# Opening columns side by side, bank evictions by ScalarE, one softmax subtraction, and a turned weight order in a gated mix of linear attention and an MLP

## The chip, the cores and the metric

The kernel runs on one core of a Trainium2 chip. The metric is the time of one execution in device microseconds. The kernel before takes 503.98 us as the median of three runs (503.89 to 505.81).

The core's engines are TensorE (PE, the products), VectorE (DVE), ScalarE (ACT), GpSimd (POOL) and SyncE (SP, which issues most DMAs). All five run their own instruction rows and wait for each other through semaphores.

## The reference

For 2048 rows x of width 512 two branches are computed and mixed by a gate.

```python
g = sigmoid((x * gate_w).sum(-1, keepdims=True))
q, k, v = split(x @ wqkv)                          # 32 heads of 16
pq, pk = q_h @ w_phi[h], k_h @ w_phi[h]            # per head, 16x16
phi = concat(softmax(p), softmax(-p))              # over the 16, for pq and pk: 32 features a head
kv, z = phi_k^T v, sum over rows of phi_k
a = (phi_q @ kv / (phi_q . z + 1e-6)) @ wo         # branch A: linear attention
b = relu(x @ w1 + b1)**2 @ w2 + b2                 # branch B: 512 -> 1792 -> 512
out = g * a + (1 - g) * b
```

Everything is float32. The two softmaxes of a row of scores need, for each head, the largest of the 16 (for +p) and the smallest (for -p).

## The kernel before, in words

**Products.** An operand is kept as two float32r tiles, a rounded high part (name ending in h) and the rest (l). A product of two such operands is three matmuls of 128x128 by 128x512: high by high, high by low, low by high (`mm3`). Where the program says "a block of twelve", it is four pairs of tiles times three. x @ w1 and x @ (wk folded, wv) use a scheme of seven products in place of eight over 2 x 2 blocks: the table `PAIRS` names them p1 to p7, tiles X... are sums of blocks of x, and O0 to O3 are the four forms of the w1 tiles.

**Phase one.** For two halves r of the rows, `u_step` makes the hidden tiles: a column u = (r, g) is seven products into the banks uA, uE and one of uB0/uB1 (shown as uB). p1 opens the bank A, ScalarE copies it to B, p2 ends A; p5 opens E, ScalarE copies it to a tile ol, p6 goes on in B, VectorE writes B + ol into E, and so on. `hidden` adds the bias, takes relu and square on ScalarE (`row<-uA,b1c`, `row<-row`), and the tile goes to DRAM (`hkept`). Two tiles of each set, made by `plain`, take the ordinary way. `v_step` does the same for keys and values with the banks vA, vB, vE; `features` makes the softmaxes of the keys, and `kv_burst` adds phi_k^T v with 64 narrow matmuls into the bank kv. `fold` multiplies w_phi into wk (and, at the end of the phase, into wq) by 64 matmuls into the four banks vA, vB, vE, kv and four transposes on VectorE (`phiT<-...`).

In the opening, column (0,1) runs p1 and p2, then column (0,2) p1 and p2, both in the bank uA; two plain tiles follow, then the fold of wk, and then the remaining products of the two columns, the second one half behind the first, ahead of the stream of later columns.

**Phase two.** It goes through the four row blocks i, in the order `ORDER_B`. For each there are 14 steps, one for each 128 rows of w2: `h_ready` loads a hidden tile into the ring (four buffers of 512, shared by nearly all loads) and splits it into O0 or O1 (`O0h<-ring` on ScalarE, `O0l<-ring,O0h` on VectorE or GpSimd, two buffers each); `w2_ready` splits a tile of w2, once, into K... tiles; `down` gives four banks (uA, uE, uB0, uB1: one for each 128 rows of the block) three matmuls each, a block of twelve. At the 14th step `evict` (line 854) empties the four banks.

Between those steps stands branch A, for pairs p of row chunks. `do_q` is the query product, a block of twelve from the folded weight (tiles XS2..., XS3..., by `wq_ready`) into one of vA, vB, vE, kv, then `exps`, `sums`. `transposed` multiplies by the normaliser (`q_phi`; GpSimd's `ez`), transposes on VectorE (`tb<-e`), and lays the pieces of tb into phiT: four by ScalarE (`phiT<-tb`), twelve by DMA. `do_n` takes phiT times kv (`vE<-phiT,kvb`), `attend` the product with wo. `gates` computes g for a block, from x in its plain form (`xn`, one buffer, four products with row sums).

`exps` (line 617) takes max and min of each head out of the bank, subtracts twice (p - max, min - p, each 512 wide) into the halves of a tile of 1024, and takes one exponential of it.

**What sets the order.** The program doesn't emit its instructions as it is written. The class `Plan` (lines 131 to 344) records each operation, gives it a due time from a clock of the products as written, and then simulates the five engines with costs of its own (`lengths`); at each step the engine that can start first takes, of the operations that could start by then, the one with the earliest due time. Operations of `nc.either` go to VectorE or GpSimd, whichever is free. PE takes products by groups, in the written order, unless the first of the next few is not ready in the simulation. A load from DRAM may start at most HORIZON (45 us) before its due time. All is then issued from one line, so that every instruction carries line 344 in the profile and is told apart by the names of its tiles.

## Time and profile before

| what | us |
|---|---|
| median of three runs | 503.98 |
| the profiled execution's own time | 505.25 |
| its span in the trace | 503.5 |
| PE busy | 490.7 (97%) |
| DVE busy | 401.9 (80%) |
| ACT busy | 245.3 (49%) |
| POOL busy | 147.6 (29%) |

The page's times are microseconds from the span's start. A row of the timeline gives start, length, engine, operation, output<-inputs, sizes, and in brackets the idle time of that engine before it with what ended it ("<-ACT row": ScalarE's write to a row). A row of the windows gives the stretch, its length, then the busy time and instruction count of PE, PEld (weight loads), DVE, ACT, POOL, and at the end the clock granted to PE (1.00 is full), the busy share of the DMA engines and GB/s. In the page's groups a row ends with the busy sum, the mean in ns, and the engine's idle time ahead of the group. Phase one lasts to about 239 us of the span, phase two from there on.

### The profile page before, as it was taken

How to read it: one execution, taken by the hardware profiler on the slowest of the kernel's cores; microseconds unless marked ns; L12 is line 12 of the kernel's file. 1: busy time of each engine (PE TensorE's matmuls, PEld its weight loads, DVE VectorE, ACT ScalarE, POOL GpSimd, SP SyncE). 2: the span in 40 equal slices, each digit the busy share in tenths (PEclk: the TensorE clock that was granted, in tenths of full speed). 3: DMA queues.
4: the chain of work that ended last, by engine and by line, in shares of the span. 5: the costliest groups of instructions: out<-in, count | busy, mean ns of one | idle time of the engine just before them, and what ended most of it. 6: DMA issues, size and time to landing. Idle time of an engine off the chain costs nothing.

```text
span 503.5 us, 9473 instructions
## 1 busy us (share of the span) xinstructions
PE 490.7 (97%) x3538; PEld 392.3 (78%) x3538; DVE 401.9 (80%) x611; ACT 245.3 (49%) x403; POOL 147.6 (29%) x122
## 2 busy tenths in 40 slices
...
GB/s 285 403 390 313 384 256 181 278 61 214 154 127 170 284 252 109 231 269 178 224 167 92 135 296 161 91 87 259 119 101 167 142 92 83 93 172 87 109 2 83
DMA packets 56518, 91.87 MB, mean 182 GB/s; under 512 B 7192, under 2 KB 16664, under 8 KB 56472
## 3 DMA queue, kind: packets, MB, share of 16 engines
...
## 4 chain that ended last, share of the span: by engine, by line
PE 74%; DMA 9%; DVE 9%; SPq 3%; ACT 2%; issue 2%; ACTq 0%; DVEq 0%
PE uB L344 20%; PE uE L344 11%; PE uA L344 11%; PE vB L344 9%; PE vA L344 8%; PE vE L344 7%; PE kv L344 7%; SPq L344 3%; DVE e L344 2%; DMA ring<-hkept 2%; DMA KT11h<-in_xT 1%; DMA b2b<-in_b 1%; ACT row L344 1%; DMA KT20h<-in_w 1%; DMA KT21l<-in_w 1%
## 5 line engine op out<-in xcount | busy, mean ns | idle before, releaser
L344 POOL TENSOR_TENSOR ez<-e,vext 128x512 f32<-128x512 f32 x32 | 44.1, 1400 | 60.8 <-ACT e L344 56.9
L344 ACT ACTIVATE O1h<-ring 128x512 fp32r<-128x512 f32 x33 | 20.7, 626 | 53.9 <-PE uB L344 25.9
L344 ACT ACTIVATE e<-e 128x1024 f32<-128x1024 f32 x27 | 28.5, 1056 | 30.9 <-DVE e L344 30.6
L344 DVE TENSOR_REDUCE sm<-e 128x64 f32<-128x1024 f32 x27 | 32.8, 1214 | 8.4 <-ACT e L344 8.3
L344 ACT ACTIVATE O0h<-ring 128x512 fp32r<-128x512 f32 x33 | 20.6, 627 | 33.5 <-PE uB L344 18.7
L344 ACT ACTIVATE row<-row 128x512 f32<-128x512 f32 x56 | 34.9, 627 | 0.8
L344 ACT ACTIVATE phiT<-tb 32x512 f32<-32x512 f32 x32 | 20.2, 630 | 26.4 <-DVE tb L344 20.3
L344 POOL TENSOR_TENSOR O0l<-ring,O0h 128x512 fp32r<-128x512 f32 x15 | 21.2, 1412 | 24.4 <-ACT O0h L344 22.8
L344 DVE TENSOR_TENSOR O1l<-ring,O1h 128x512 fp32r<-128x512 f32 x22 | 18.2, 829 | 12.3 <-ACT O1h L344 12.2
L344 POOL TENSOR_TENSOR O1l<-ring,O1h 128x512 fp32r<-128x512 f32 x11 | 14.2, 1292 | 27.9 <-ACT O1h L344 20.0
L344 DVE TENSOR_TENSOR O0l<-ring,O0h 128x512 fp32r<-128x512 f32 x18 | 14.3, 792 | 8.3 <-ACT O0h L344 8.3
L344 DVE TENSOR_TENSOR e<-e,w 128x1024 f32<-128x1024 f32 x16 | 20.2, 1261 | 0.2
L344 DVE TENSOR_REDUCE dz<-ez 128x64 f32<-128x1024 f32 x16 | 19.2, 1201 | 0.9 <-POOL ez L344 0.9
L344 DVE STREAM_TRANSPOSE tb<-e 128x1024 f32<-128x1024 f32 x16 | 19.7, 1232 | 0.1
L344 DVE SCALAR_TENSOR_TENSOR xn<-xn,gwb 128x512 f32<-128x512 f32 x16 | 13.5, 843 | 7.1 <-DMA xn<-in_xn 6.3
L344 DVE RECIPROCAL r<-sm 128x64 f32<-128x64 f32 x32 | 17.5, 546 | 0.5
L344 POOL TENSOR_TENSOR ring<-ring,ring 128x256 f32<-128x256 f32 x5 | 5.0, 1002 | 41.5 <-DVE O0l L344 24.8
L344 DVE TENSOR_TENSOR e<-e,r 128x1024 f32<-128x1024 f32 x11 | 16.8, 1523 | 0.2
L344 DVE TENSOR_REDUCE mx<-vA 128x32 f32<-128x512 f32 x10 | 6.9, 687 | 11.4 <-PE vA L344 11.4
L344 POOL TENSOR_TENSOR ring<-ring 128x256 f32<-128x256 f32 x3 | 3.2, 1068 | 40.9 <-DMA ring<-in_w 40.9
L344 DVE TENSOR_REDUCE mx<-vB 128x32 f32<-128x512 f32 x14 | 9.5, 676 | 6.0 <-PE vB L344 6.0
L344 ACT ACTIVATE row<-row,b1c 128x512 f32<-128x512 f32 x13 | 9.3, 719 | 7.8 <-DVE row L344 7.8
...
## 6 DMA issues: line engine op xcount, KB each, us to landing
...
```

The lines of the kernel that those rows point to most:

```text
L344: call(*map(real, op.args), **{k: real(a) for k, a in op.kw.items()})
```

## The change

- *Opening*: columns (0,1) and (0,2) run side by side, product by product; the second one uses vB and vE in place of uA and uE. The third and fourth weight forms of column 2 lie in two tiles apart (`ASIDE`). The fold of wk comes behind the first two items of the later columns, in place of ahead of the first p5.
- *Gates*: loads of xn are no longer held to the horizon of 45 us.
- *Softmax*: `exps` makes one subtraction of 1024 that reads the bank twice by broadcast (p - max and p - min), and two exponentials of 512, the second with the factor -1.
- *Second phase*: the 14 tiles of w2 and of the hidden layer are taken in the order 2, 3, ..., 13, 0, 1 (`turned`).
- *Evictions*: a finished bank is copied by ScalarE, into the row or (with the factor 1-g) into a slot of the ring, and the addition follows on VectorE or GpSimd, from SBUF. The very last block adds from the bank as before.
- *Planner*: where VectorE or ScalarE would take an operation that is due over 5 us later, it looks for one that becomes ready while that would run and is due soon, and takes that first, waiting for it.

```diff
--- before.py
+++ after.py
@@ -155,7 +155,7 @@
         writes = [aps[0]] + ([kw["accum_out"]] if outs == 2 else [])
         reads = [a for a in aps[1:] if a is not kw.get("accum_out")]
         op.size = max(free_size(a) for a in aps)
-        op.early = method == "dma_start" and reads[0].space == DRAM
+        op.early = method == "dma_start" and reads[0].space == DRAM and reads[0].tensor.name != "in_xn"
         wide = [a for a in reads if free_size(a) > 1]
         op.two = method in ("tensor_tensor", "scalar_tensor_tensor") and len(wide) > 1 and all(a.space != PSUM for a in wide)
         for a in reads:
@@ -331,6 +331,12 @@
                 if s <= t + 1e-9:
                     able.append(op)
             op = min(able, key=lambda o: (o.due, o.n))
+            if e in ("vector", "scalar") and op.due > t + 5.0:
+                ahead = t + self.lengths(op, e)[1]
+                soon = [o for o in waiting[e] if t < o.ready < ahead and o.due < o.ready + 1.0]
+                if soon and op.method != "dma_start":
+                    op = min(soon, key=lambda o: (o.due, o.n))
+                    t = max(free[e], op.ready, lock if op.two else 0.0)
             for x in op.choices:
                 waiting[x].remove(op)
             launch(op, e, t)
@@ -464,10 +470,14 @@
 
 
 
-    def w_tiles(i):
+    def w_tiles(i, g=None):
+        if (g, i) in ASIDE:
+            return [operand(t)[:, :512 if i < 3 else 256] for t in ASIDE[g, i]]
         if i < 2:
             return [operand(f"O{i}{j}", 512, 2) for j in "hl"]
         return [operand(f"O{i}{j}", 512 if i == 2 else 256) for j in "hl"]
+
+    ASIDE = {(2, 2): ("KB211l", "KT31l"), (2, 3): ("KT21h", "KB111l")}
 
     def w_kept(g, i, j):
         return wkept4[g, j] if i == 3 else wkept[g, i, j]
@@ -489,7 +499,7 @@
     def w_ready(r, g, i):
         if (r, g, i) in st:
             return
-        t = st[r, g, i] = w_tiles(i)
+        t = st[r, g, i] = w_tiles(i, g if r == 0 else None)
         if r == 1 and g > 0:
             for j in range(2):
                 nc.sync.dma_start(ff(t[j]), w_kept(g, i, j))
@@ -527,7 +537,7 @@
     def u_step(u, p):
         r, g = u
         if p == "p1":
-            st["A", u] = banks["uA"]
+            st["A", u] = banks["vB" if u == (0, 2) else "uA"]
             uproduct(st["A", u], u, p, True, False)
             st["B", u] = turn("uB0", "uB1")
             nc.scalar.activation(st["B", u], st["A", u], AF.Copy)
@@ -535,7 +545,7 @@
             uproduct(st["A", u], u, p, False, True)
             hidden(2 * r, 2 * g, st["A", u])
         elif p == "p5":
-            st["E", u] = banks["uE"]
+            st["E", u] = banks["vE" if u == (0, 2) else "uE"]
             uproduct(st["E", u], u, p, True, False)
             t = st["t5", u] = buf("ol", 512, 2)
             nc.scalar.activation(t, st["E", u], AF.Copy)
@@ -616,15 +626,15 @@
 
     def exps(ps, tag="e"):
         pv = ps.rearrange("p (h f) -> p h f", f=DH)
-        mx, mn = small("mx", H), small("mn", H)
+        ends = small("ends", 2 * H).rearrange("p (h t) -> p h t", t=2)
         ef = buf(tag, 2 * D, 2 if tag == "e" else 1)
         e = ef.rearrange("p (h t f) -> p h t f", t=2, f=DH)
-        bc = lambda t: t.unsqueeze(2).to_broadcast([P, H, DH])
-        nc.vector.tensor_reduce(mx, pv, AX.X, ALU.max)
-        nc.vector.tensor_reduce(mn, pv, AX.X, ALU.min)
-        nc.vector.tensor_tensor(e[:, :, 0, :], pv, bc(mx), ALU.subtract)
-        nc.vector.tensor_tensor(e[:, :, 1, :], bc(mn), pv, ALU.subtract)
-        nc.scalar.activation(ef, ef, AF.Exp)
+        for t, op in enumerate((ALU.max, ALU.min)):
+            nc.vector.tensor_reduce(ends[:, :, t], pv, AX.X, op)
+        nc.vector.tensor_tensor(e, pv.unsqueeze(2).to_broadcast([P, H, 2, DH]), ends.unsqueeze(3).to_broadcast([P, H, 2, DH]),
+                                ALU.subtract)
+        for t, scale in enumerate((1.0, -1.0)):
+            nc.scalar.activation(e[:, :, t, :], e[:, :, t, :], AF.Exp, scale=scale)
         return ef.rearrange("p (h f) -> p h f", f=DH)
 
     def sums(e3):
@@ -750,6 +760,10 @@
             split(t, *hl, nc.either)
             st.setdefault("wb", []).append(hl)
 
+    def turned(f):
+
+        return (f + 2) % NF
+
     def w2_place(f, j):
         return f"K{KOPS[f // 2]}{f % 2}{j}"
 
@@ -757,14 +771,15 @@
 
         if ("w2", f) in st:
             return
-        src = load(slot(w2_place(f + 1, "l")) if f < NF - 1 else ring(), w2[f * P:(f + 1) * P, :])
+        src = load(slot(w2_place(f + 1, "l")) if f < NF - 1 else ring(), w2[turned(f) * P:(turned(f) + 1) * P, :])
         t = st["w2", f] = [operand(w2_place(f, j)) for j in "hl"]
         split(src, *t, nc.either)
 
     def h_ready(t):
         i, f = divmod(t, NF)
         hi, lo = st["h", t] = [operand(f"O{t % 2}{j}", 512, 2) for j in "hl"]
-        split(load(ring(), hkept[ORDER_B[i], f]), hi, lo, nc.either)
+        b, f = ORDER_B[i], turned(f)
+        split(load(ring(), hkept[b, f]), hi, lo, nc.either)
 
     def q_phi(n, e3, r):
         ez = buf("ez", 2 * D).rearrange("p (h f) -> p h f", f=DH)
@@ -851,13 +866,18 @@
         mm3(st["d"][c], st["h", t], st["w2", f], slice(c * P, (c + 1) * P), ALL, f == 0,
             f == NF - 1 or t == NB * NF - 3 and c == NC - 1)
 
-    def evict(n, d, s):
-        if ("f", n) in st:
+    def evict(n, d, s, last=False):
+        if ("f", n) not in st:
+            o = st["f", n] = row()
+            nc.scalar.activation(o, d, AF.Copy)
+            nc.either.tensor_tensor(o, o, st["b2b"], ALU.add)
+        elif last:
             o = st["f", n]
             nc.vector.scalar_tensor_tensor(o[:, s], d[:, s], rest[:, n:n + 1], o[:, s], ALU.mult, ALU.add)
         else:
-            o = st["f", n] = row()
-            nc.vector.tensor_tensor(o, d, st["b2b"], ALU.add)
+            t, o = ring(), st["f", n]
+            nc.scalar.activation(t, d, AF.Copy, scale=rest[:, n:n + 1])
+            nc.either.tensor_tensor(o, o, t, ALU.add)
 
 
 
@@ -890,9 +910,6 @@
                 x_split(0, op, kk)
         plain(1, 1, banks["vE"])
         plain(1, 0, banks["kv"])
-        wph = load(slot("KT40h"), wphi)
-        fold("k", wkT, [slot(t) for t in ("KT40l", "KT41h", "KT41l", "KB220h")], wph)
-        fetch_v()
         for kk in range(2):
             x_sums(0, kk)
 
@@ -943,14 +960,17 @@
     U1, U2 = (0, 1), (0, 2)
     x_ready(0, "S3")
     x_ready(0, "S4")
-    us = [(U1, "p5"), (U1, "p6"), (U1, "p7"), (U1, "p3"), (U2, "p5"), (U1, "p4"), (U2, "p6"), (U2, "p7"), (U2, "p3")]
-    us += u_stream([(0, g) for g in range(3, NPF)], U2)
-    run(us[:16])
+    run([(U1, "p5"), (U1, "p6"), (U2, "p5"), (U2, "p6"), (U1, "p7"), (U2, "p7"), (U1, "p3"), (U1, "p4"), (U2, "p3")])
+    us = u_stream([(0, g) for g in range(3, NPF)], U2)
+    run(us[:2])
+    fold("k", wkT, [slot(t) for t in ("KT40l", "KT41h", "KT41l", "KB220h")], load(slot("KT40h"), wphi))
+    fetch_v()
+    run(us[2:12])
     for op in ("B11", "T1", "T3", "B22", "T2", "B21", "T4"):
         for kk in range(2):
             k_ready(op, kk)
     vs = v_stream([(0, m, "kv") for m in range(NC)])
-    run(merged(us[16:], vs))
+    run(merged(us[12:], vs))
 
     x_fetch(1)
     x_fetch2(1)
@@ -1016,10 +1036,10 @@
             continue
         for c in range(NC):
             n = ORDER_B[i] * NC + c
-            evict(n, st["d"][c], ALL)
+            evict(n, st["d"][c], ALL, last)
             if last and c == NC - 1:
                 for e, d, s in zip((nc.sync, nc.scalar), ends, halves):
-                    evict(n, d, s)
+                    evict(n, d, s, last)
                     e.dma_start(out[n * P:(n + 1) * P, s], st["f", n][:, s])
             else:
                 out_done(n)
```

PE in the opening, where the first two columns begin. The names: uA, vB, vE are banks, XA... tiles of x (half 0 is row block A11, XA12 is A12), O0 and O1 the weight forms; a number behind _ counts versions (different ones are different contents). Before:

```order
L344 MATMUL vE<-XA221l_228,O1h_156 128x512
L344 MATMUL vE<-XA221h_217,O1l_158 128x512
L344 MATMUL uA<-XA120h_149,O0h_172 128x512
L344 MATMUL uA<-XA120l_152,O0h_172 128x512
L344 MATMUL uA<-XA120h_149,O0l_186 128x512
L344 MATMUL uA<-XA121h_163,O0h_172 128x512
L344 MATMUL uA<-XA121l_167,O0h_172 128x512
L344 MATMUL uA<-XA121h_163,O0l_186 128x512
L344 MATMUL uA<-XA110h_134,O0h_165 128x512
L344 MATMUL uA<-XA110l_138,O0h_165 128x512
```

And in the changed kernel, at the same part of the program:

```order
L350 MATMUL uA<-XA111h_140,O0h_172 128x512
L350 MATMUL uA<-XA111l_145,O0h_172 128x512
L350 MATMUL uA<-XA111h_140,O0l_185 128x512
L350 MATMUL vB<-XA110h_134,O0h_165 128x512
L350 MATMUL vB<-XA110l_138,O0h_165 128x512
L350 MATMUL vB<-XA110h_134,O0l_177 128x512
L350 MATMUL vB<-XA111h_140,O0h_165 128x512
L350 MATMUL vB<-XA111l_145,O0h_165 128x512
L350 MATMUL vB<-XA111h_140,O0l_177 128x512
L350 MATMUL uA<-XA120h_149,O0h_172 128x512
L350 MATMUL uA<-XA120l_152,O0h_172 128x512
```

The other column's first six matmuls now go to vB and stand between the first and the second six of the column in uA; before, both columns took uA one after the other.

PE where the phases meet: the last products of phase one (uB), the last burst (kv, 32 matmuls for each of two row chunks), and what follows. XS2... is the folded query weight, KB110 the first tile of w2 that is used, O0 its hidden tile. Before:

```order
L344 MATMUL uB_72<-XA221h_1583,O3l_2745 128x512
L344 MATMUL kv<-ez_2542,vext_98 32x32 x32
L344 MATMUL kv<-e_2738,vext_99 32x32 x32
L344 MATMUL vA<-XS20h_2959,XA110h_1371 128x512
L344 MATMUL vA<-XS20l_2967,XA110h_1371 128x512
```

In the changed kernel:

```order
L350 MATMUL uB_72<-XA221h_1569,O3l_2737 128x512
L350 MATMUL kv<-ez_2526,vext_98 32x32 x32
L350 MATMUL kv<-e_2718,vext_99 32x32 x32
L350 MATMUL uA<-KB110h_2488,O0h_2846 128x512
L350 MATMUL uA<-KB110l_2495,O0h_2846 128x512
L350 MATMUL uA<-KB110h_2488,O0l_2855 128x512
L350 MATMUL uE<-KB110h_2488,O0h_2846 128x512
L350 MATMUL uE<-KB110l_2495,O0h_2846 128x512
L350 MATMUL uE<-KB110h_2488,O0l_2855 128x512
L350 MATMUL uB_72<-KB110h_2488,O0h_2846 128x512
```

Behind the burst the first tile's block of twelve comes ahead of the first query product, where the query product came first; the rows on vA follow behind the six of uB_72 and uB_73.

The evictions at the end of the first row block. VectorE before (row is the output tile, rest is 1-g, b2b the bias, tb, dz, sm, mx parts of branch A):

```order
L344 TENSOR_REDUCE dz_3567<-ez_3533 128x64
L344 SCALAR_TENSOR_TENSOR row_3542<-uA,rest,row_3542 128x512
L344 TENSOR_TENSOR row_3582<-uE,b2b_3036 128x512
L344 TENSOR_TENSOR row_3588<-uB_72,b2b_3036 128x512
L344 TENSOR_TENSOR row_3596<-uB_73,b2b_3036 128x512
L344 TENSOR_REDUCE mx_3605<-vB 128x32
```

ScalarE in the changed kernel:

```order
L350 ACTIVATE e_3476<-e_3476 128x32x16 x2
L350 ACTIVATE phiT_3525<-tb_3450 32x2x256 x4
L350 ACTIVATE ring_3551<-uA,rest 128x512
L350 ACTIVATE row_3557<-uE 128x512
L350 ACTIVATE row_3566<-uB_72 128x512
L350 ACTIVATE row_3572<-uB_73 128x512
L350 ACTIVATE e_3562<-e_3562 128x32x16 x2
```

The four banks leave by ScalarE, behind two exponentials and four copies of a transposed tile, where VectorE emptied them behind branch A's reductions.

## The prediction, made before the changed kernel had run

> **What bounds the kernel now.** I read the page first: the busy row of its first part.
>
> ```profile
> span 503.5 us, 9473 instructions
> PE 490.7 (97%) x3538; PEld 392.3 (78%) x3538; DVE 401.9 (80%) x611; ACT 245.3 (49%) x403; POOL 147.6 (29%) x122
> ```
>
> TensorE (PE) is busy 97% of the span, and the change takes no product away. So all it can win lies in the 12.8 us in which PE does nothing, and in the time in which PE works slowly. Next, therefore, the timeline of PE. Its rows with idle time in brackets are all the waits after the first microsecond.
>
> ```profile
> 19.25 0.50 PE L344 MATMUL uA<-XA110h,O0h 128*128 128x512 f32 x1 [1.59 <-ACT row L344]
> 30.62 0.50 PE L344 MATMUL uB<-XS30h,O2h 128*128 128x512 f32 x1 [0.86 <-DVE uE L344]
> 48.45 0.50 PE L344 MATMUL uB<-XS30h,O2h 128*128 128x512 f32 x1 [1.12 <-DVE uE L344]
> 238.28 0.76 PE L344 MATMUL kv<-e,vext 128*32 128x32 f32 x64 [0.41 <-DVE e L344]
> 240.89 0.80 PE L344 MATMUL vA<-XS20h,XA110h 128*128 128x512 f32 x1 [1.85 <-ACT XS20h L344]
> 287.97 0.37 PE L344 MATMUL vE<-phiT,kvb 64*32 64x256 f32 x1 [1.89 <-DMA phiT<-tb]
> 377.33 0.47 PE L344 MATMUL uA<-KB110h,O0h 128*128 128x512 f32 x1 [0.79 <-DVE row L344]
> ```
>
> Seven waits: 3.57 us in the opening, 2.26 where the two phases meet, 1.89 at the first transposed pair, 0.79 at the second end of a block: 8.51 us. The other 4.3 us stand at the two ends of the program, which the change leaves alone. Then the windows, for the granted clock (the PEclk number, third from the right).
>
> ```profile
> 240.00:246.00 6.00, 5.10 (x11) 3.72 (x12) 4.75 (x8) 4.24 (x8) 0.00 (x0) 0.56 0.76 223
> 246.00:252.00 6.00, 6.00 (x25) 4.80 (x25) 4.81 (x10) 2.37 (x4) 3.03 (x2) 0.88 0.71 196
> 288.00:294.00 6.00, 6.00 (x45) 4.26 (x46) 6.00 (x8) 1.60 (x3) 1.07 (x1) 0.72 0.89 297
> ```
>
> Behind the two longest waits the clock falls. The loss is (1 - 0.56) x 6 + (1 - 0.88) x 6 = 3.36 us behind the wait of 1.85, and (1 - 0.72) x 6 = 1.68 us behind that of 1.89. Behind 1.59 it doesn't fall. So a ceiling follows: 8.51 + 3.36 + 1.68 = 13.55 us, if every wait goes and none comes.
>
> The unit for all that follows is a block of twelve products, from the chain of waits: 2.74 us, or 0.228 a product.
>
> ```profile
> 299.04 2.76 PE vA L344 x12
> 301.80 2.73 PE vB L344 x12
> ```
>
> **The opening.** Its waits are for single-bank reuse and for VectorE (DVE).
>
> ```profile
> 18.52 0.68 ACT L344 ACTIVATE row<-uA,b1c 128x512 f32<-128x512 f32 x1
> 28.96 0.68 DVE L344 STREAM_TRANSPOSE phiT<-kv 128x512 f32<-128x512 f32 x1
> 29.87 0.70 DVE L344 TENSOR_TENSOR uE<-uB,ol 128x512 f32<-128x512 f32 x1 [0.23 <-PE uB L344]
> 47.71 0.69 DVE L344 TENSOR_TENSOR uE<-uB,ol 128x512 f32<-128x512 f32 x1
> ```
>
> The first: column two can't begin in uA until ScalarE (ACT) has read column one (18.52 + 0.68). Now it lies in vB, and between two touches of a bank by PE stand six products of the other column, 1.37 us, or more: gone. The second and third: a bank uB gets its next product only after DVE's addition, one row later on PE. With two columns side by side, another column's product stands between, 1.37 us against waits of 0.86 and 1.12: gone. What is new: the fold (64 rows) moves behind the first two columns, and its four transposes, some 2.4 us on DVE, now hold up the additions there. I walked PE from 8.90 at 0.228 a product: the fold falls at about 38, its transposes end at about 43, and the copy uB<-uA of the fifth column, queued on ACT behind the first split of the folded weight, comes about 0.5 us late near 49. Bounds: 0, and 1.59 (the longest wait of this stretch). Term: 3.57 - 0.5 = 3.1. The loads of w_phi and wk that move back on SP's queue are needed 12 us later than before, those of w1 that move up come sooner; they cost nothing, and if one were late it would show as a wait on DMA ahead of the fold.
>
> **Where the phases meet.** Before, PE's next work is the query product on the folded weight, whose last transpose, split and subtraction are these:
>
> ```profile
> 239.29 0.67 DVE L344 STREAM_TRANSPOSE phiT<-vE 128x512 f32<-128x512 f32 x1
> 239.70 0.61 ACT L344 ACTIVATE O1h<-ring 128x512 fp32r<-128x512 f32 x1
> 240.22 0.61 ACT L344 ACTIVATE XS20h<-phiT 128x512 fp32r<-128x512 f32 x1
> 240.96 0.68 DVE L344 TENSOR_TENSOR XS20l<-phiT,XS20h 128x512 fp32r<-128x512 f32 x1
> 243.28 0.63 ACT L344 ACTIVATE O0h<-ring 128x512 fp32r<-128x512 f32 x1 [0.88 <-DMA ring<-hkept]
> 234.56 1.30 POOL L344 TENSOR_TENSOR O0l<-ring,O0h 128x512 fp32r<-128x512 f32 x1 [1.62 <-DMA KT41l<-in_w]
> 236.71 0.61 ACT L344 ACTIVATE KT40h<-KT41l 128x512 fp32r<-128x512 f32 x1
> ```
>
> The other work, the first hidden tile, came only at 243.28, because it was the last one written. With tile three first, that tile was written long ago; its split stands on ACT where KT40h stood (236.71), its subtraction on POOL takes 1.30, so it is there at about 239.0, just when the second burst ends (it starts at 238.28, lasts 0.76, and loses its wait of 0.41: between 238.6 and 239.0). Twelve products, 2.74 us, then cover the query's wait of 1.85. KB221l leaves DVE's row ahead of the scaled e, so the 0.41 goes too. With the wait its clock loss goes. New: up to 0.6 if the POOL half is late; I take 0.3. Term: 2.26 + 3.36 - 0.3 = 5.3.
>
> The Trainium skill ("TensorE: Matmul & The Clock Gate", Part 1, What's actually happening) says that the array falls to half rate after an idle window of about 3.4 us, on a free-running window. The lengths agree (6.7 and 3.4 us at half clock by the windows above), the threshold doesn't: gaps of 1.85 and 1.89 were enough, and the trace decides.
>
> **The first transposed pair.** PE gets to it later by one query block and sooner by one tile: from the end of the first query product 11 tiles and 3 queries stand before it, now 10 and 4, 14 blocks either way. So the chain to it must become shorter by itself.
>
> ```profile
> 246.13 0.63 PE L344 MATMUL vA<-XS31h,XA121l 128*128 128x512 f32 x1
> 258.25 0.63 ACT L344 ACTIVATE O1h<-ring 128x512 fp32r<-128x512 f32 x1 [4.44 <-DMA ring<-hkept]
> 258.92 0.79 DVE L344 TENSOR_TENSOR O1l<-ring,O1h 128x512 fp32r<-128x512 f32 x1 [3.18 <-ACT O1h L344]
> 277.39 1.23 DVE L344 STREAM_TRANSPOSE tb<-e 128x1024 f32<-128x1024 f32 x1
> 278.65 7.78 SPq L344 DMA_DIRECT2D phiT<-tb  x12
> ```
>
> It ran from 246.8 to 288.0. PE came at 286.08 (287.97 less its wait of 1.89), so 1.9 us must go. DVE stood 3.18 us in it behind a split that waited for its load; the tiles now are read earlier, being older. Against that, one gate product more lies inside it (about 0.9 us, row below), and ACT does each exponential in two pieces. Net 3.18 - 0.9 - 0.3 = 2.0 shorter, give or take 2 us for pairs on DVE and POOL that stretch one another: on the edge. All of 1.89 + 1.68 = 3.57 or nothing; I take 2.5.
>
> **Softmax, gates, evictions.**
>
> ```profile
> L344 ACT ACTIVATE e<-e 128x1024 f32<-128x1024 f32 x27 | 28.5, 1056 | 30.9 <-DVE e L344 30.6
> L344 DVE TENSOR_REDUCE sm<-e 128x64 f32<-128x1024 f32 x27 | 32.8, 1214 | 8.4 <-ACT e L344 8.3
> L344 DVE SCALAR_TENSOR_TENSOR xn<-xn,gwb 128x512 f32<-128x512 f32 x16 | 13.5, 843 | 7.1 <-DMA xn<-in_xn 6.3
> 375.30 1.22 DVE L344 TENSOR_TENSOR e<-e,w 128x1024 f32<-128x1024 f32 x1
> 376.44 0.74 DVE L344 SCALAR_TENSOR_TENSOR row<-uA,rest,row 128x512 f32<-128x512 f32 x1
> 290.17 0.58 ACT L344 ACTIVATE oh<-vB 128x512 fp32r<-128x512 f32 x1
> ```
>
> Two subtractions of 512 become one of 1024. The trace has none out of a bank; the nearest is the reduction of 1024, 1.21, against 2 x 0.60 from start to start: nothing either way. Two exponentials of 512 cost 0.1 to 0.2 more than one, on an engine busy 49%. The gates are the same sixteen products, earlier; POOL and SP cover nothing new. The eviction that made PE wait stood behind e<-e,w on DVE; on ACT it is a copy of 0.58, for 12 of the 16, and the addition behind it holds no bank. ACT has nothing of length ahead of it at that end of a block: 0.7 of 0.79. Each copy with a factor takes a slot of the ring of four, which can hold back one load; the loads run some tiles ahead, and that hides it.
>
> For waits that a walk by hand misses, in 440 us of new order, I take off 1.0 (0 to 3; seven waits of 1.2 on average stood before).
>
> **Sum:** 3.1 + 5.3 + 2.5 + 0.7 - 1.0 = 10.6 us. The profiled execution took 505.25 with a span of 503.5; it would be 494.65. Its time lies 1.27 above the median of 503.98, so the median becomes 493.4.
>
> **The rivals.**
>
> 1. The transposed pair still waits (chance 0.20). For it: DVE is the chain, and the copies by SP alone take 7.78 us. Without that term, 8.1 us: 495.9.
> 2. The opening is DVE's (0.12). DVE and ACT are both full there, so the waits move instead of going. Against it: the walk finds the operands ready. Without 3.1: 496.5.
> 3. The clock falls anyway (0.08), since the narrow products of the kv burst count for little. The gap of 1.59 without a fall, and bursts elsewhere at full clock, speak against it. Without 3.36 and with 1.0 less of the third term: 497.8. By the skill's page named above, gaps this short are no cause at all, which is this rival.
> 4. Slower (0.05): PE waits for ACT at each end of a block. Ahead of the evictions ACT now has in turn four copies that wait for DVE, a split that waits for a load, and two exponentials.
>
> ```profile
> 302.32 2.57 ACT L344 ACTIVATE phiT<-tb 32x512 f32<-32x512 f32 x4 [2.79 <-DVE tb L344]
> ```
>
> Behind uA's last product PE has an attend block of twelve (2.74 us) and the nine products of the other three banks (9 x 0.228 = 2.05) before it reaches uA again. If ACT is later than that by 2 us, the clock falls for two stretches (3.36): three ends cost 3 x 5.36 = 16 us, so 503.98 - 10.6 + 16 = 509. It decides from a lateness of 1.9 us on. By the walk ACT is 2 us early.
> 5. The change does not do what it says (0.06): the older tile is not split in time because its O0 buffer is still held by the last weight tile, and small waits eat the rest: 502 to 506.
>
> **How the numbers follow.** Forecast 0.49, rivals as above. A measurement of this kernel tells about 0.5%, 2.5 us, from no change. Faster: 0.49 + 0.20 + 0.12 + 0.08 = 0.89; same 0.06; slower 0.05. The range starts at the ceiling, 503.98 - 13.55 = 490.4, and goes up past rivals 1 to 3 with 1.5 us more of unknown waits: 499.3. Left out are rivals 4 and 5 and a little of 3.
>
> **What would show it.** Right: no PE row with idle between 9 and 37; uA<-KB110h straight behind the second burst and PEclk 1.00 from 240 on; uA at the second end of a block without a wait on DVE. Wrong step by step: a wait on ACT or DVE near 49 over 1 us (opening); PE waiting for POOL's O0l, or PEclk below 1 behind the burst (meeting); vB<-phiT waiting on DMA (third term); uA<-KB110h waiting on ACT (rival 4). Several new waits near 2 us with falls of the clock would make the forecast wrong as a whole.

## The result

The changed kernel takes 501.89 us as the median of 17 runs (499.84 to 504.34), the kernel before 504.44 us beside it: a ratio of 0.9932, with an interval of 0.9912 to 0.9953. Forecast were 493.4 us and a range of 490.4 to 499.3. It is faster, by 0.7%, a quarter of what was forecast (2.5 us of 10.6). Timed once more, later, the ratio was 0.9923 (0.9897 to 0.9948).

The profiled execution took 501.8 us, with this span and these busy times in the first part of the page:

```profile
span 500.0 us, 9484 instructions
PE 487.1 (97%) x3538; PEld 390.9 (78%) x3538; DVE 396.6 (79%) x572; ACT 254.6 (51%) x447; POOL 153.1 (31%) x129
```

These are all of its waits on PE behind the first microsecond, from PE's timeline, and the windows with a low clock:

```profile
30.96 0.50 PE L350 MATMUL uB<-XS30h,KB211l 128*128 128x512 f32 x1 [0.69 <-DVE vE L350]
282.57 0.59 PE L350 MATMUL vB<-phiT,kvb 64*32 64x256 f32 x2 [3.77 <-DMA phiT<-tb]
286.24 0.60 PE L350 MATMUL vE<-phiT,kvb 64*32 64x256 f32 x1 [3.08 <-DMA phiT<-tb]
338.85 0.37 PE L350 MATMUL vE<-phiT,kvb 64*32 64x256 f32 x1 [1.36 <-DVE den L350]
...
282.00:288.00 6.00, 2.35 (x32) 0.89 (x32) 5.97 (x10) 0.15 (x1) 2.40 (x2) 0.59 0.54 154
288.00:294.00 6.00, 6.00 (x29) 4.83 (x23) 5.34 (x11) 2.08 (x4) 2.58 (x2) 0.84 0.92 308
```

Three things are to be seen. Of the opening's three waits one of 0.69 is left. Where the phases meet, PE has no wait and no window below full clock. At the first transposed pair PE waits 3.77 and 3.08, 6.85 us in place of 1.89, and a pair further on waits 1.36. The waits are 8.90 us in sum, against 8.51 before: what went in the first half of the program came back in the second.

By the forecast's own terms (waits from the rows; for the clock, PE's busy time in each half-microsecond window between 230 and 310 us, times what the clock lacks, which makes 4.98 us before and 1.91 now):

| term | forecast, us | measured, us |
|---|---|---|
| opening | 3.1 | 3.57 - 0.69 = 2.88 |
| meeting of the phases, with its clock | 5.3 | 2.26 + 3.3 = 5.6 |
| first pair, with its clock | 2.5 | 1.89 - 6.85 + 1.68 - 1.91 = -5.2 |
| end of a block | 0.7 | 0.79 |
| waits not foreseen | -1.0 | -1.36 |
| sum | 10.6 | 2.7 (3.45 between the two executions) |

One term of five is wrong, by 7.7 us, and it has the other sign.

### The profile page after: what moved, and what is told of

The parts are those of the page before. It is cut to its first block, busy times and chain, and to the rows that moved or that the text cites. A ratio compares the mean times of both kernels' runs of the same rounds, so it can differ in the third digit from the quotient of the medians.

```text
span 500.0 us, 9484 instructions
## 1 busy us (share of the span) xinstructions
PE 487.1 (97%) x3538; PEld 390.9 (78%) x3538; DVE 396.6 (79%) x572; ACT 254.6 (51%) x447; POOL 153.1 (31%) x129
## 4 chain that ended last, share of the span: by engine, by line
PE 80%; DVE 7%; DMA 7%; ACT 2%; SPq 2%; issue 1%; POOL 0%; ACTq 0%; DVEq 0%; POOLq 0%
PE uB L350 21%; PE uA L350 12%; PE uE L350 12%; PE vB L350 11%; PE vA L350 9%; PE vE L350 9%; PE kv L350 6%; DMA row<-in_wo 2%; SPq L350 2%; DMA KT11l<-in_xT 1%; DVE e L350 1%; DMA wkept<-O0l 1%; DMA vext<-zrow 1%; DMA tb<-in_xT 1%; ACT row L350 1%
## 5 line engine op out<-in xcount | busy, mean ns | idle before, releaser
L350 POOL TENSOR_TENSOR O1l<-ring,O1h 128x512 fp32r<-128x512 f32 x15 | 19.8, 1319 | 93.3 <-ACT O1h L350 92.5
L350 ACT ACTIVATE e<-e 128x512 f32<-128x512 f32 x54 | 31.4, 622 | 28.9 <-DVE e L350 28.9
L350 ACT ACTIVATE O1h<-ring 128x512 fp32r<-128x512 f32 x33 | 20.7, 627 | 39.3 <-PE uB L350 13.4
L350 ACT ACTIVATE row<-row 128x512 f32<-128x512 f32 x56 | 34.2, 626 | 0.6
L350 POOL TENSOR_TENSOR O0l<-ring,O0h 128x512 fp32r<-128x512 f32 x14 | 19.3, 1379 | 35.4 <-ACT O0h L350 35.4
L350 DVE TENSOR_REDUCE ends<-vB 128x32 f32<-128x512 f32 x28 | 18.0, 680 | 8.7 <-PE vB L350 8.7
L350 DVE TENSOR_REDUCE ends<-vA 128x32 f32<-128x512 f32 x20 | 12.8, 681 | 10.2 <-PE vA L350 10.0
L350 DVE TENSOR_TENSOR e<-vB,ends 128x1024 f32<-128x1024 f32 x12 | 14.4, 1203 | 0.2
L350 DVE TENSOR_TENSOR e<-e,r 128x1024 f32<-128x1024 f32 x11 | 14.5, 1323 | 0.1
L350 DVE SCALAR_TENSOR_TENSOR xn<-xn,gwb 128x512 f32<-128x512 f32 x16 | 11.8, 736 | 1.2 <-DMA xn<-in_xn 1.2
L350 ACT ACTIVATE row<-uB,b1c 128x512 f32<-128x512 f32 x13 | 8.8, 680 | 6.9 <-PE uB L350 6.9
L350 ACT ACTIVATE row<-uA,b1c 128x512 f32<-128x512 f32 x13 | 8.9, 681 | 6.2 <-PE uA L350 6.1
```

The source lines that it names most:

```text
L350: call(*map(real, op.args), **{k: real(a) for k, a in op.kw.items()})
```

## Where the gain went

The chain to the pair starts with the first query product and runs through VectorE to the second transpose (`tb<-e`), and from there through SP's twelve copies to PE. The last part costs the same as ever: from the end of the second transpose to PE's row 9.35 us before, 9.33 now, most of it SP's issuing. (The wait of 1.36 at the third pair is named after VectorE's den, which had ended at 338.50, and it too ends 9.5 us behind that pair's second transpose, which ends at 329.31: by its place it is a wait for the copies.)

```profile
276.93 7.77 SPq L350 DMA_DIRECT2D phiT<-tb  x12
```

The first part grew. From the first query product's last row to the end of the second transpose it took 278.62 - 246.13 = 32.5 us before and 276.91 - 240.07 = 36.8 now. The windows of that stretch, first of the kernel before, then of the changed one, tell of what (the columns are PE, PEld, DVE, ACT, POOL):

```profile
246.78:278.62 31.84, 31.84 (x141) 26.24 (x141) 27.96 (x40) 11.42 (x17) 17.51 (x14) 0.99 0.46 140
```

```profile
240.50:276.91 36.41, 36.41 (x163) 30.13 (x162) 33.99 (x45) 11.54 (x21) 21.06 (x16) 1.00 0.45 139
```

VectorE is busy 33.99 us in place of 27.96, and idle 2.4 in place of 3.9. The groups of VectorE's rows in the same stretch show which. Before:

```profile
L344 DVE TENSOR_TENSOR e<-e,w 128x1024 f32<-128x1024 f32 x2 | 2.4, 1214 | 0.0
L344 DVE SCALAR_TENSOR_TENSOR den<-dz,eps 128x32 f32<-128x32 f32 x2 | 1.9, 947 | 0.0
L344 DVE SCALAR_TENSOR_TENSOR dz<-dz,inv,r 128x64 f32<-128x64 f32 x2 | 1.8, 908 | 0.0
L344 DVE TENSOR_TENSOR w<-r,den 128x64 f32<-128x64 f32 x2 | 0.4, 216 | 0.0
```

In the changed kernel:

```profile
L350 DVE TENSOR_TENSOR e<-e,w 128x1024 f32<-128x1024 f32 x2 | 3.4, 1712 | 0.0
L350 DVE SCALAR_TENSOR_TENSOR dz<-dz,inv,r 128x64 f32<-128x64 f32 x2 | 2.6, 1315 | 0.0
L350 DVE TENSOR_TENSOR w<-r,den 128x64 f32<-128x64 f32 x2 | 2.3, 1169 | 0.0
L350 DVE TENSOR_SCALAR inv<-ge 128x4 f32<-128x4 f32 x1 | 1.3, 1271 | 0.1
L350 DVE TENSOR_SCALAR eps<-inv 128x4 f32<-128x4 f32 x1 | 1.1, 1070 | 0.0
L350 DVE SCALAR_TENSOR_TENSOR xn<-xn,gwb 128x512 f32<-128x512 f32 x1 | 0.7, 676 | 0.0
L350 DVE SCALAR_TENSOR_TENSOR den<-dz,eps 128x32 f32<-128x32 f32 x2 | 0.5, 240 | 0.0
```

The gates bring 3.45 us (inv, eps, xn, and three short rows of 0.42), where the forecast had 0.9: the first block's gates, done at 233 us before the change, now end at 247, in the chain. The pair's own rows bring 2.3 more (e, dz and w longer by 3.7, den shorter by 1.4), and that is a matter of where they meet GpSimd. From the timelines of both engines:

```profile
262.08 1.29 POOL L350 TENSOR_TENSOR XS10l<-ring,XS10h 128x512 fp32r<-128x512 f32 x1 [2.80 <-ACT XS10h L350]
262.11 1.34 DVE L350 TENSOR_TENSOR w<-r,den 128x64 f32<-128x64 f32 x1
...
273.25 1.29 POOL L350 TENSOR_TENSOR ez<-e,vext 128x512 f32<-128x512 f32 x1
273.41 2.22 DVE L350 TENSOR_TENSOR e<-e,w 128x1024 f32<-128x1024 f32 x1
```

A row of 64 elements that takes 0.2 alone ends when GpSimd's does, after 1.34; one of 1024, which takes 1.2 alone, ends 1.1 behind GpSimd's. The Trainium skill ("SBUF — State Buffer", SBUF: two separate sides) states a port pair that VectorE and GpSimd share as an exclusive lock, held for a whole instruction, and these rows agree.

Two rows more are to be seen at the head of the chain, ScalarE's and GpSimd's:

```profile
249.28 0.63 ACT L350 ACTIVATE wo<-row 128x512 fp32r<-128x512 f32 x1 [1.75 <-DMA row<-in_wo]
249.99 1.29 POOL L350 TENSOR_TENSOR O2l<-row,wo 128x512 fp32r<-128x512 f32 x1 [5.51 <-ACT wo L350]
251.26 2.54 POOL L350 TENSOR_TENSOR ez<-e,vext 128x512 f32<-128x512 f32 x2
```

GpSimd's `ez`, which the chain needs, stood behind a split of wo that waited for its load.

Two theories were put to the chip. One: **the pair's chain is VectorE's, made of its own rows, of those that other work puts among them, and of their collisions, and it sets the time there; what PE does less behind the chain's start is only a longer wait**. The other: **any edit makes the planner order VectorE's rows anew, and the waits of the second phase are drawn again**, so a single part has no gain of its own there. The first asks for edits that keep the order, the second for edits that mean nothing.

## Experiments on single parts

For each kernel below, this is what the chain did: the start of the first query product's last row, the end of the second transpose, their distance, and the waits of the first pair's rows on PE.

| kernel | last query row | second transpose ends | distance | waits at the first pair |
|---|---|---|---|---|
| before | 246.13 | 278.62 | 32.5 | 1.89 |
| changed | 240.07 | 276.91 | 36.8 | 3.77 + 3.08 |
| b_opening | 241.24 | 275.60 | 34.4 | 1.14 + 3.26 |
| b_turned | 246.10 | 280.33 | 34.2 | 0.84 + 3.40 |
| a_gates_held | 239.47 | 270.36 | 30.9 | 0.35 + 3.41 |
| a_no_lookahead | 246.00 | 278.69 | 32.7 | 2.52 + 2.99 |
| b_horizon46 | 247.17 | 283.58 | 36.4 | 1.68 |
| a_horizon46 | 242.07 | 275.85 | 33.8 | 3.14 + 2.58 |

**The opening alone** (b_opening), on the kernel before:

```diff
-        st["A", u] = banks["uA"]
+        st["A", u] = banks["vB" if u == (0, 2) else "uA"]
...
-    us = [(U1, "p5"), (U1, "p6"), (U1, "p7"), (U1, "p3"), (U2, "p5"), ...]
+    run([(U1, "p5"), (U1, "p6"), (U2, "p5"), (U2, "p6"), (U1, "p7"), (U2, "p7"), ...])
+    run(us[:2])
+    fold("k", wkT, ...)
```

> The kernel before with the new opening alone. Theory (the chain to the first transposed pair sets the time behind the meeting of the phases, counted from the end of the first query product): the waits of 1.59, 0.86 and 1.12 us go but for 0.7, 2.9 us; the meeting and the pair keep their waits of 2.26 and 1.89 and their clock loss, since the chain begins with the query product and moves with it. So 504.4 - 2.9 = 501.5. Rival (the pair is held by something that does not move with PE, the loads on SP's queue): the pair's wait grows from 1.89 to about 4.8 and the time stays within 1 us of before.

Measured: 505.38 us, ratio 1.0012 (0.9984 to 1.004). The opening's waits went as forecast, to 0.19 and 0.24, and the meeting's shrank to 1.31 without a fall of the clock. All of it is gone by the end of the second block:

```profile
238.81 0.50 PE L344 MATMUL vA<-XS20l,XA110h 128*128 128x512 f32 x1 [1.31 <-DVE XS20l L344]
281.11 0.59 PE L344 MATMUL vB<-phiT,kvb 64*32 64x256 f32 x2 [1.14 <-DMA phiT<-tb]
284.95 0.60 PE L344 MATMUL vE<-phiT,kvb 64*32 64x256 f32 x1 [3.26 <-DMA phiT<-tb]
377.37 0.47 PE L344 MATMUL uA<-KB110h,O0h 128*128 128x512 f32 x1 [2.73 <-DVE row L344]
```

PE came to the pair at 281.11 - 1.14 = 279.97, 5.5 us sooner than before the change, the pair's last operand only 3.0 sooner. The rival's numbers came (4.4 at the pair, no gain), not its reason: the chain did move with the query product, and was 1.9 us longer.

**The order of w2 alone** (b_turned), on the kernel before:

```diff
-        src = load(..., w2[f * P:(f + 1) * P, :])
+        src = load(..., w2[(f + 2) % NF * P:((f + 2) % NF + 1) * P, :])
...
-        split(load(ring(), hkept[ORDER_B[i], f]), hi, lo, nc.either)
+        split(load(ring(), hkept[ORDER_B[i], (f + 2) % NF]), hi, lo, nc.either)
```

> The kernel before with the order of w2 turned by two tiles alone. Theory (chain counted from the end of the first query product, its length set by VectorE's work): the waits of 0.41 and 1.85 and the clock loss of 3.36 behind them go, 5.6 us; the pair waits 0 to 4 us, as its 41.2 us from the query product to the pair stay. Time 497 to 501. Rival (the chain is anchored ahead of the query product): the pair comes at the same time after the bursts as before, its wait grows by 5 us to about 7, and the time stays within 1 us of before, 503.5 to 505.

Measured: 510.48 us, ratio 1.0117 (1.0088 to 1.0147), slower, which neither had expected. The waits of the meeting went, 0 in place of 2.26. But 1.80 us came up ahead of the fold of wq, 4.24 at the pair, and 4.38 at the second end of a block, with a fall of the clock behind it. In the changed kernel the same part stands without the first and the last of these.

**The gates held back** (a_gates_held), on the changed kernel:

```diff
-        op.early = method == "dma_start" and reads[0].space == DRAM and reads[0].tensor.name != "in_xn"
+        op.early = method == "dma_start" and reads[0].space == DRAM
```

> The changed kernel with the loads of xn held to 45 us again. Theory (VectorE's work between the first query product and the pair grew by 6.0 us, 3.45 of it rows of the gates): those rows go ahead of the query product or behind the pair, the pair's waits of 3.77 and 3.08 shrink by 2 to 3.5 us, time 501.9 - 3 = 499. Rival (other work of VectorE moves into the place that the gates leave, or the collisions with GpSimd alone matter): the waits stay within 1.5 us of 6.85 and the time within 1 us of 501.9.

Measured: 506.84 us, ratio 1.0051 (1.0021 to 1.0082). At the pair the theory's number came, 3.76 in place of 6.85, the chain 5.9 us shorter, but not by its reason. The small rows of the first block's gates stand in the chain as they do in the changed kernel, behind the last query row at 239.47, and end at 247.76. From VectorE's timeline:

```profile
242.10 1.26 DVE L350 TENSOR_SCALAR inv<-ge 128x4 f32<-128x4 f32 x1 [0.45 <-ACT ge L350]
244.47 0.64 DVE L350 TENSOR_SCALAR eps<-inv 128x4 f32<-128x4 f32 x1
247.59 0.17 DVE L350 TENSOR_SCALAR rest<-ge 128x4 f32<-128x4 f32 x1
```

Only the product of the second block went out, to behind the second transpose (xn at 271.99): the gates bring 2.25 us in place of 3.45. VectorE is busy 27.55 us from the last query row to that transpose's end, in place of 34.42, so most of the 5.9 us are other rows that were drawn anew, and the number was met by luck. The time did not follow either, since 2.51 us came up at the second end of a block ("<-ACT ring") and 2.75 + 0.90 at 450 us, and the clock, summed as in the table of terms but over the whole span, lost 5.7 us in place of 1.9.

**Without the planner's look-ahead** (a_no_lookahead), on the changed kernel:

```diff
-            if e in ("vector", "scalar") and op.due > t + 5.0:
-                ahead = t + self.lengths(op, e)[1]
-                soon = [o for o in waiting[e] if t < o.ready < ahead and o.due < o.ready + 1.0]
...
```

> The changed kernel without the planner's look-ahead rule on VectorE and ScalarE. Theory (the gain of single parts is lost to waits that come up elsewhere, since any edit orders VectorE anew): at least two waits over 1 us stand at other places than 282.57, 286.24 and 338.85, and the time is 500 to 508, without a rule on the sign. Rival (look-ahead is what held VectorE up ahead of the pair): the pair's waits shrink by over 3 us with no new wait over 1 us elsewhere, 497 to 499.

Measured: 511.15 us, ratio 1.0114 (1.0087 to 1.014), 3 us beyond the theory's range. The pair still waits 5.51. The two new waits are for ScalarE's evictions:

```profile
375.67 0.50 PE L344 MATMUL uA<-KB110h,O0h 128*128 128x512 f32 x1 [1.88 <-ACT ring L344]
381.16 0.79 PE L344 MATMUL uE<-KB110h,O0h 128*128 128x512 f32 x1 [4.51 <-ACT ring L344]
```

So the look-ahead is not what held the pair up. The plan without it is 9.3 us slower, and evictions that come late on ScalarE account for as much: 6.4 us of waits, and 2.9 us of clock behind them.

**A number that means nothing** (b_horizon46 on the kernel before, a_horizon46 on the changed one):

```diff
-HORIZON = 45.0
+HORIZON = 46.0
```

> The kernel before with one number of the planner changed, the horizon of early loads from 45 to 46 us, which should mean nothing to any engine. Theory (the order of VectorE's rows is redrawn by any edit, and the waits of the second phase with it): the waits of the opening stay (1.59, 0.86, 1.12), those from 230 us on change by more than 2 us in sum, and the time moves by over 1 us up or down from 504.4. Rival (the plan is steady and the changes of the single parts are their own): the same seven waits to within 0.3 us, time within 1 us of 504.4.

> The changed kernel with the planner's horizon at 46 us in place of 45. Theory (order redrawn by any edit): the opening keeps its single wait of 0.7 or less, the waits from 230 us on (3.77, 3.08, 1.36) change by more than 2 us in sum, the time moves by over 1 us from 501.9. Rival (steady plan): the same waits to within 0.3 us and 501.9 within 1 us.

Measured: the kernel before became slower, 507.72 us (ratio 1.0051, 1.0027 to 1.0075). The changed kernel kept its time, 502.40 (0.9942, 0.9918 to 0.9966). About a quarter of VectorE's rows stand in another order in each. Before the change, from 230 us on, eight waits with 6.8 us in sum stand where four with 4.9 stood, at other places, of which these are two:

```profile
240.08 0.75 PE L344 MATMUL kv<-e,vext 128*32 128x32 f32 x64 [1.58 <-DVE e L344]
293.13 0.37 PE L344 MATMUL vE<-phiT,kvb 64*32 64x256 f32 x1 [1.68 <-DMA phiT<-tb]
```

In the changed one the pair still waits 5.7 and the 1.36 further on is gone. The theory asked for 2 us in the waits of both and 1 us in the time of both; it got 1.9 and 2.5 in the waits, and the time of one. The opening's waits moved by 0.13 at most in either: redrawing reaches the second phase. So an edit through this planner can move the time by 2.8 us (507.72 - 504.92) for no reason of its own, as much as the whole change is worth. What one part alone is worth in the second phase can't be had from kernels that the planner orders anew.

**The pair two tiles later, by the program** (a_pair_2later), on the changed kernel:

```diff
-            when(at[2 * p + c] + 2 + 2 * c, transposed, p, c)
+            when(at[2 * p + c] + 2 + 2 * c + (1 if (p, c) == (1, 1) else 0), transposed, p, c)
...
-        when(s + (9 if p == 0 else 8), do_n, p)
+        when(s + (11 if p == 0 else 8), do_n, p)
-            when(s + 11 + c, attend, p, c)
+            when(s + (12 if p == 0 else 11) + c, attend, p, c)
```

> The changed kernel with the first pair's products two tiles later on PE, and what follows from it one tile later (the last transposed chunk of the second pair is written one step later too, since it needs the same tile). Theory (PE merely has nothing to do while the pair's chain runs): two blocks of twelve, 5.5 us, go into the wait of 6.85; 1.4 is left and the clock stays up: 501.9 - 5.5 - 1.5 = about 495. Rival (the plan gives the chain later due times and VectorE does it later by as much): waits still over 5 us, time 501 to 503.

Measured: 498.90 us, ratio 0.9894 (0.9862 to 0.9926), between the two forecasts. The pair has no wait at all. This doesn't show that the two tiles filled it, for the chain was drawn anew as well: 28.9 us from the last query row (245.57) to the end of the second transpose (274.49), in place of 36.8. And the meeting has a wait again, for the GpSimd half of the first tile's split, which the forecast had named as its risk there and had put at 0.6 at most, and the third pair waits:

```profile
235.78 0.79 PE L350 MATMUL uA<-KB110h,O0l 128*128 128x512 f32 x1 [2.78 <-POOL O0l L350]
335.48 0.37 PE L350 MATMUL vE<-phiT,kvb 64*32 64x256 f32 x1 [2.31 <-DMA phiT<-tb]
```

**The wait filled with products of ones** (a_pair_fill), on the changed kernel:

```diff
+        one = lambda n: nc.const_aps.tensor(1.0, (P, n), mybir.dt.bfloat16)
+        for _ in range(30 if p == 0 else 0):
+            nc.tensor.matmul(pss[0], one(P), one(512), start=True, stop=True)
```

> The changed kernel with thirty products of ones (bfloat16, 128x512) ahead of the first pair's products on PE, in the bank that these overwrite: 30 x 0.228 = 6.8 us of work that nothing needs. Theory (the pair's chain sets the time there and not PE, and the clock falls because PE stands idle): the waits of 3.77 and 3.08 are filled, the pair's products come at the same time, the clock stays at 1.00 behind them, and the loss of about 1.8 us (3.66 us of products at half rate) goes: 501.9 - 1.8 = 500.1. Rival 1 (PE does set the time): the added products cost up to 6.8 us, 504 or more. Rival 2 (the clock falls for another reason, such as the narrow products of the pair): no gain, 501.9, and a clock of 0.5 behind the pair.

Measured: 506.53 us, ratio 1.0014 (0.9988 to 1.004), by its time rival 1. By its place it is the theory: the products fill the wait, the pair's rows follow with 0.40, and the clock stays at 1.00 behind them. The row that waits 0.40 starts 9.5 us behind the second transpose's end (278.44; 9.3 to 9.8 us in the other kernels), so the added work did not hold it up.

```profile
280.26 6.73 PE L350 MATMUL vB<-const-bfloat16-1.0 128*128 128x512 bf16 x30
286.93 0.62 PE L350 MATMUL vB<-phiT,kvb 64*32 64x256 f32 x2
287.94 0.37 PE L350 MATMUL vE<-phiT,kvb 64*32 64x256 f32 x1 [0.40 <-issue]
...
288.00:294.00 6.00, 6.00 (x52) 4.63 (x53) 5.96 (x11) 2.73 (x6) 2.23 (x2) 1.00 0.64 209
```

Against that stand 0.83 and 0.91 ahead of the pair, 0.95 at an end of a block and 3.46 at 451.76, all new, for the products moved the plan.

## Experiments with the order kept

For the rest, the plan of the changed kernel was kept as it is, and rows were moved by hand in it. `by_hand` takes each engine's rows in the planner's order and moves those that it names; the others keep their order.

```diff
-        for op in self.order():
+        for op in by_hand(self, self.order()):
...
+def behind(seq, ops, last):
+    """in one engine's order: ops, as they stand, to just behind last"""
```

In the table, two waits joined by + stand at one pair.

| kernel | moved | us | ratio to before | waits on PE from 50 us on |
|---|---|---|---|---|
| changed | nothing | 501.89 | 0.9932 (0.9912 to 0.9953) | 3.77 + 3.08, 1.36 |
| f_pair | pair behind three tiles | 511.20 | 1.0138 (1.0106 to 1.0170) | 14.16, 2.33 |
| f_gates | gates out of the chain | 500.40 | 0.9913 (0.9875 to 0.9951) | 1.62 + 3.19, 2.31 |
| f_ez | ez ahead of O2l | 499.08 | 0.9899 (0.9866 to 0.9932) | 1.41 + 3.09 |
| f_all | the three, third pair a tile later | 508.97 | 1.0106 (1.0059 to 1.0154) | 0.67, 13.83, 1.04 |
| f_pair_b | pair behind two tiles, evictions ahead | 499.73 | 0.9894 (0.9859 to 0.9928) | 1.49, 0.43 + 3.41 |
| f_gates_ez | gates and ez | 500.56 | 0.9902 (0.9866 to 0.9938) | 0.68, 0.61 + 3.18 |
| f_best | all, pair as in f_pair_b | 498.13 | 0.9879 (0.9838 to 0.9919) | 3.24, 0.96 |
| f_best2 | and second pair behind a query | 496.81 | 0.9845 (0.9823 to 0.9867) | 0.27, 0.84, 1.90, 0.19, 1.13 |

**What the chain is made of** (f_gates, f_ez, f_gates_ez). Of GpSimd's row and of VectorE's:

```diff
 TENSOR_TENSOR XS40l<-row,XS40h 128x512
-TENSOR_TENSOR O2l<-row,wo_0 128x512
 TENSOR_TENSOR ez<-e,vext_98 128x512
 TENSOR_TENSOR ez<-e,vext_99 128x512
+TENSOR_TENSOR O2l<-row,wo_0 128x512
...
 STREAM_TRANSPOSE phiT<-vE 128x4x4x32
+TENSOR_SCALAR inv<-ge 128x4
+TENSOR_SCALAR eps<-inv 128x4
...
-SCALAR_TENSOR_TENSOR xn,lg<-xn,gwb 128x512
-TENSOR_SCALAR inv<-ge 128x4
 TENSOR_REDUCE ends<-vA 128x32 x2
-TENSOR_SCALAR eps<-inv 128x4
```

> The changed kernel with every order kept, but the rows of the gates taken out of the pair's chain: the fourth product of the first block's gates and its four small rows to where VectorE still serves phase one (ahead of the first query product), the first product of the second block's gates to behind the pair's second transpose, with its next load behind the twelve copies. Theory A (VectorE's sum of work from the first query product to the second transpose sets the chain): 3.4 us less work, the pair comes 3 us sooner, the waits shrink from 6.85 to about 3.8, time 498.5. Theory B (the chain is held at its start by GpSimd's ez, which stands behind a split of wo that waits for its load): only the 0.75 behind ez counts, the waits shrink by 1 us or less, time 501 to 502.

> The changed kernel with every order kept, but GpSimd's first two ez rows ahead of the split of wo (O2l) that they stood behind. Theory A (VectorE's sum of work): ez comes up to 3 us sooner (248.3 in place of 251.3), VectorE's idle 1.77 ahead of dz goes and no more, the waits shrink by 1 to 1.8, time 500.5. Theory B (held at its start): the pair comes 3 us sooner, waits 3.9, time 498.5. If neither, VectorE is met by more collisions with GpSimd and the pair comes when it did.

> The changed kernel with every order kept, but the gates' rows out of the pair's chain and ez ahead of O2l, both. Theory (VectorE's sum of work up to the second transpose): the two gains of 2.4 and 1.7 us add up to 4.1, the pair's waits sink to 2.7, time 497 to 498 if the third pair's wait stays under 1.4. Rival (one limit behind both, the landing of the broadcast that ez reads): together no more than 2.5 us sooner, waits over 4, time 499 to 500.

From the last query row to the second transpose's end it is 34.8 us in f_gates, 34.5 in f_ez and 33.8 in f_gates_ez, against 36.8 (36.8 again, 276.48 - 239.73 = 36.75, where the changed kernel was profiled once more). So each is worth 2.0 to 2.4. Theory A had 3 for the gates and 1 to 1.8 for ez, theory B under 1 and 3: neither is right for both, A is nearer. In f_gates VectorE's work in the chain fell by 3.4 (31.03 us busy in place of 34.42), as planned, but its idle time grew by 1.3: it waits 2.1 for ez, where it waited 1.8, and 0.6 for a split. So the chain became 2.1 shorter and not 3.4. In f_ez the wait for ez shrank from 1.8 to 0.3. Together the two edits shorten it by 3.1, less than their sum of 4.4, and the pair's waits are 3.79 where the theory had 2.7 and the rival over 4. The times of the three lie within each other's intervals, and each of these overlaps the changed kernel's: what is shown is the place of the waits, not a gain in time.

**Work put into the wait** (f_pair, f_all, then f_pair_b). The order of PE's blocks (T a tile, n the pair's products, a attend, q query):

```diff
-n T T a q T a T T n
+T T T n T a q a T n
```

> The changed kernel with every engine's order kept as it is, but on PE the first pair's products three tiles later (two tiles of 12 and one of 12 that stood behind it now stand ahead; the attend and query blocks follow behind the next tile). Nothing else is moved, so no order is redrawn. Theory (PE only lacks work while the pair's chain runs): 8.2 us of work fill the waits of 3.77 and 3.08, the pair's products begin without a wait, the clock stays up, and 6.85 + 1.8 go, less up to 1 for attend blocks that now come sooner behind their splits: 501.9 - 8 = 494. Rival (the chain is stretched by PE's own work, or the tiles brought forward are not split in time): a wait of 2 us or more stands on the tiles' O operands or still on the pair, time over 498.

> The three edits of order in one kernel (the first pair three tiles later, the gates' rows out of its chain, ez ahead of O2l), and the third pair's products one tile later as well, for its wait of 1.36. Theory: no wait over 0.7 us is left on PE, so 501.9 less 6.85, 1.8 and 1.36, about 492. Rival: new waits come up at the end of a block, where the evictions now stand nearer to the pair, and the time is no better than with the first edit alone.

The pair's products began without a wait, in both. But the third tile is the last one of its row block, and so PE stood in front of that block's evictions instead, for 14 us. In f_pair neither forecast had that place, and its time is far from the theory's; f_all's rival had the place. From ScalarE's and PE's timelines of f_pair:

```profile
298.68 2.54 ACT L352 ACTIVATE phiT<-tb 32x512 f32<-32x512 f32 x4 [3.01 <-DVE tb L352]
301.23 0.69 ACT L352 ACTIVATE ring<-uA,rest 128x512 f32<-128x512 f32 x1
...
301.97 0.79 PE L352 MATMUL uA<-KB110h,O0h 128*128 128x512 f32 x1 [14.16 <-ACT ring L352]
```

The eviction is a row of 0.69, but it stands on ScalarE behind the second pair's copies, and these wait for VectorE. This is the forecast's fourth rival, with its place and its mechanism; in the changed kernel itself PE comes late enough for it. In f_pair_b the last tile of the block stays behind the pair, and the four evictions go ahead of the rows they stood behind:

```diff
-ACTIVATE e<-e 128x32x16 x2
-ACTIVATE phiT<-tb 32x2x256 x4
 ACTIVATE ring<-uA,rest 128x512
...
 ACTIVATE row<-uB_73 128x512
+ACTIVATE e<-e 128x32x16 x2
+ACTIVATE phiT<-tb 32x2x256 x4
```

> The changed kernel with every order kept, but on PE the first pair's products two tiles later (the last tile of the block stays behind them, now ahead of the first attend block), and on ScalarE the four evictions of that block ahead of the two exponentials and four copies that they stood behind. Theory A (the wait can be filled, and the 14 us at the end of the block came from ScalarE's row alone): the pair waits 1.4 to 2 in place of 6.85, the evictions make PE wait under 1, the clock falls once at most: 496 to 497. Theory B (VectorE's chains set the whole stretch up to the second pair, and PE's gain moves from wait to wait): the second pair, whose copies now come behind the evictions, waits 3 us or more, time 500 to 503.

Measured: 1.49 at the first pair, none at the block's end, and then 0.43 + 3.41 at the second pair, with a fall of the clock. Both of A's places came, and then B's: the wait moves on. The time lies in neither range. The second pair's wait is not made by the copies that now stand behind the evictions: its second transpose ends at 298.82, as in the changed kernel (298.62), and PE's row starts 9.5 us later, at 308.36. In the changed kernel PE comes there at 311.05, so of a wait filled at the first pair only some 3 us can be won before the second pair holds PE. At 499.73 us it is some 2 us better than the changed kernel by the medians, not 5.5, and the two intervals overlap.

**All of it** (f_best, f_best2):

> All of it: the gates' rows out, ez ahead, the first pair two tiles later with the evictions ahead of the copies, and the third pair one tile later. Theory A: no wait over 0.8 on PE, no fall of the clock, 501.9 - 6.85 - 1.8 - 1.36 = 492. Theory B (the gain moves on to the next wait of VectorE's chain): a new wait of over 2 us at the second or the third pair or at the end of a block, 496 or more.

> All of the edits of order in the last kernel (gates out, ez ahead, first pair two tiles later with the evictions ahead of the copies, third pair one tile later) and the second pair's products behind the query block that followed them. Theory A: its wait of 3.24 shrinks by that block's 2.74 to 0.5, the clock stays up, 498.1 - 2.74 - 1 = about 494.5. Theory B (the gain moves on): a wait of over 2 us at the third pair or at the end of the second block, 497 to 499.

f_best has no wait at the first pair and 3.24 at the second, which is theory B. The profile names VectorE's row as what ended it, but VectorE had read that bank by 297.07, and the wait ended at 306.02, 9.6 us behind the second transpose (296.44): it is the pair's copies again. f_best2 puts the second pair's products behind the next query block and ends with this, from PE's timeline and the windows:

```profile
306.96 0.37 PE L352 MATMUL vA<-phiT,kvb 64*32 64x256 f32 x1 [0.84 <-issue]
335.30 0.37 PE L352 MATMUL vE<-phiT,kvb 64*32 64x256 f32 x1 [1.90 <-DVE den L352]
...
332.00:336.00 4.00, 2.10 (x29) 1.09 (x34) 3.18 (x6) 1.30 (x3) 2.49 (x2) 0.95 0.56 129
336.00:340.00 4.00, 4.00 (x31) 2.63 (x17) 4.00 (x6) 1.60 (x3) 1.24 (x1) 0.62 0.84 263
```

At the second pair theory A's 0.5 nearly came; at the third pair 1.90 came up, just under theory B's 2 (it ends behind the copies too, which SP issues from 325.83 to 333.46), and the time lies between the two forecasts, next to B's. It is faster than both kernels: 496.81 us, against 504.62 before and 500.50 for the changed kernel, timed beside it, and its interval lies below the changed kernel's (0.9897 to 0.9948).

> The changed kernel unaltered, on the same chip and against the same runs of the kernel before. Every theory expects the ratio that it had, 0.993 within its interval (0.991 to 0.995), and the waits of 3.77 and 3.08 at the first pair to within 1 us.

The unaltered kernel gave 0.9923 and waits of 3.69 and 2.65, within the bounds.

Of the two theories, the first holds at the first pair: rows taken out of VectorE's chain shorten the pair's waits, and work added on PE ahead of it does not delay it. Its limit is that the next pair waits instead. The second holds for each of the edits here that went through the planner.

## Why the prediction was wrong

- **Opening, right.** Forecast 3.1, measured 2.88. Its waits (9 to 50 us) sank to under 1 us in sum in every kernel with the new opening. The wait near 49 that the walk gave as 0.5 is not there in the changed kernel (0.24 and 0.25 in two others); the one that is there, 0.69 at 30.96, the walk had missed.
- **Meeting of the phases, right.** Forecast 5.3, measured 5.6. The tile was there, PE went from the burst into it, and the clock stayed up. That the POOL half can be late was the named risk, and in a plan drawn anew it cost 2.78, not 0.6.
- **First pair, wrong, and with it the whole.** The step that failed is "the chain to it must become shorter by itself ... net 2.0 shorter", "all of 1.89 + 1.68 = 3.57 or nothing". The chain became 4.3 us longer (41.8 to 46.2 from the last query row to the pair's last operand). Of its three sizes, the gate rows were 3.45 and not 0.9, and VectorE's idle time shrank by 1.5 and not 3.18, for another wait took the place, that for ez. The third, "give or take 2 us for pairs on DVE and POOL", was 2.3 and all on one side. And "nothing" was no bound: a chain can grow as well as shrink, and then the wait grows with it. It grew by 4.96, which is 4.3 of chain and 0.6 by which PE's own way to the pair became shorter (from the last query row 286.08 - 246.13 = 39.95 before, 282.57 - 3.77 + 0.6 - 240.07 = 39.3 now, the 0.6 being the pair's rows ahead of the second wait). A floor at the old wait was assumed, without a row for it.
- **Rival 1** said that the pair still waits, at its old price: 495.9. It had the mechanism and the reason (VectorE is the chain, and SP's copies take 7.78) and the wrong size. **Rival 3**, no gain at the clock, did not come where the phases meet; at the pair a fall stayed (1.91), behind waits that stayed too. **Rival 4** did not come in the changed kernel, but came when other things were moved: 2.51 in a_gates_held, 6.4 in a_no_lookahead, 14 in f_pair and f_all. **Rival 2** and rival 5 did not come.
- **End of a block, right**: 0.79 went, 0.7 was forecast. **Waits not foreseen**: 1.36, where 1.0 was taken.
- **The chances.** 0.89 on faster by over 0.5% fits what was measured; the range did not, since each edge was built from terms that had a floor at zero, while a redrawn order can lose as well as win.

Open is why the planner put the first block's gates into the chain. That it did is in the rows. The earlier loads are not the reason by themselves: with the loads held (a_gates_held) the gates still end at 247.76, and with the horizon at 46 and the loads let go (a_horizon46) they are done at 225. Which of the change's parts moved them is not shown. Nor were the eviction by ScalarE and the single subtraction tried alone, since a kernel that is ordered anew would not have told their worth; in the chain itself three subtractions of 1024 take 3.65 us where six of 512 took 4.02, so that part did not lengthen it. That the collisions with GpSimd cost 2.3 us is read from the rows; no kernel took them away alone.
